# Windowed attention with a gated feed-forward layer on one core: the second product turned round, in blocks of 128 tokens over pairs of batches

## The chip, the cores and the metric

The kernel runs on one core of a Trainium2 chip. The core has a matrix engine (TensorE, PE in the profile, its weight loads PEld), three engines for elementwise work (VectorE = DVE, ScalarE = ACT, GpSimd = POOL) and a queue engine, SyncE (SP), that issues transfers. The metric is the device time in microseconds of one execution. The time before is the median of three runs, 547.44 us (547.39 to 547.52). The profile is of one execution, whose first and last instruction lie 546.0 us apart.

## What is computed

Eight batches of 576 tokens, eight heads of 64. The first four heads attend to the last 32 tokens, the others to every fourth of the last 128. The heads' outputs side by side are the input x (512 columns) of a feed-forward layer with 1024 inner columns:

```
def _attn_ref(q, k, v):                      # B, H, S, D = 8, 8, 576, 64
    scores = scale * np.matmul(q, k.transpose(0, 1, 3, 2))
    mask_plain = (rel >= 0) & (rel < window)                               # window 32
    mask_dil = (rel >= 0) & (rel < window * dilation) & (rel % dilation == 0)   # dilation 4
    attn = softmax(np.where(masks, scores, -1e9))
    return np.matmul(attn, v)

def _moe_ref(x, w_in, conv_w, w_out):        # x: 8 x 576 x 512, d_ff 1024
    h = np.maximum(x @ w_in, 0.0)
    conv_out = sum(conv_w[k] * hp[:, k:k + S, :] for k in range(3))   # hp: h with a zero at each end of the tokens
    gate = 1.0 / (1.0 + np.exp(-conv_out))
    return (h * gate @ w_out).astype(np.float32)
```

## The kernel before, in words

Work is cut into tasks, and a planner (class Planner, L76) puts them in order before the program is written. Each task has an engine, an estimated cost, a due time, a function that writes its instructions, the tasks that it comes after, and the buffers that it uses. The planner keeps a model of when each engine is free; among the tasks that could start within 0.25 us of the earliest on an engine it takes the one with the smallest due time. Due times are therefore priorities, and their scale matters only against each other. A buffer is taken from a pool of slots when its first task is placed and goes back when its last task is done. The order of each engine's instructions in the program is the order that comes out.

**Attention** (attention, L235) makes one task chain for each pair of heads, four pairs a batch. SP loads queries and keys (L243) and values (L245). PE forms the scores (L264) in the one accumulator "att"; for the first eight pairs a mask product goes ahead (L253), and VectorE and ScalarE make maxima and nine exponentials with their sums (L274 to L284); for the others VectorE adds the mask (L289, L292) and ScalarE makes one exponential (L298). VectorE normalizes and transposes (L305, L307), PE multiplies by the values (L318), and ScalarE and VectorE write the result as a high part (L368) and a rest (L384). Seven slots "x" hold these results, one pair each.

**The weights** (weights, L462) are split into a high part and a rest as well, in chunks of 128 x 512: eight of w_in, eight of w_out. GpSimd's queue loads the raw words into an "out" slot (L470), ScalarE and VectorE work on them (L477 to L512), and for nine chunks PE adds the parts (L499 to L501). The chunks' due times are WI and WO.

**The feed-forward layer** (expert, L391) runs once a batch. All its products take three matmuls for each chunk of the contraction: high by high, high by rest, rest by high (TERMS, L389).

- The first product (L402) has w_in stationary and 288 tokens moving: for each of the eight inner chunks fc and each half of the tokens, 4 x 3 matmuls into a PSUM slot "mm". ScalarE applies the relu and writes h (L409).
- Gating of chunk fc: ScalarE multiplies by the middle tap (L420), VectorE adds the other two (L414), ScalarE takes the sigmoid (L425), VectorE multiplies by h (L427), ScalarE writes the high part of the gated activations g (L429), VectorE the rest (L431). h and c have three slots each; g has eight, one for each chunk, so that a batch's g can be written only when the batch before has read that slot for the last time.
- The second product (L444) has w_out stationary and 288 tokens of g moving. For each of four blocks dm of 128 output columns and each half of the tokens, eight tasks k of three matmuls each run into a PSUM slot "nn" (two slots). Chunk 2 dm + k // 4 of w_out belongs to block dm, so a block needs two chunks of w_out and all eight of g. ScalarE copies the half out (L451), and SP stores a block of 128 x 576 (L458; for the last batch, each half by itself). The result lies transposed in memory, columns by tokens, and is put right on the host.

DUE gives each batch three due times, for the first product, the gating and the second product; PAIR gives one for each pair of heads; for batches 2 to 7 both follow a period of 57.4 us.

Of the kernel before, what the change touches and what calls it, by code (L numbers as in the profile page):

```python
# [8 lines left out]
F32 = mybir.dt.float32  # L36
F32R = mybir.dt.float32r
# [4 lines left out]
ALU = mybir.AluOpType  # L42
AX = mybir.AxisListType

B, H, S, D = 8, 8, 576, 64
DM, DF = 512, 1024
# [4 lines left out]
HALF = S // 2  # L51
RUNS = ((0, 5), (5, 9), (9, 14), (14, 18))
NC, NF = DM // 128, DF // 128
# [3 lines left out]
SCALE = 1.0 / D ** 0.5  # L57
ONE = dict(start=True, stop=True, skip_group_check=True)
# [101 lines left out]
def attn_moe(ctx: ExitStack, tc: tile.TileContext, qk_p, qk_d, v_p, v_d, w_in, w_out, conv, mask, out):  # L160
    nc = tc.nc
# [10 lines left out]
    wo = [[const.tile([128, 512], F32R, name=f"wo{j}{c}") for c in range(2 * NC)] for j in range(2)]  # L172
# [15 lines left out]
    slots("g", NF, [128, S], F32R, 2)  # L188
# [13 lines left out]
    AHEAD = (8.0, 4.1, 0.0)  # L202
# [186 lines left out]
    TERMS = ((0, 0), (0, 1), (1, 0))  # L389

    def expert(b, ready, wired, wored, conved):  # L391
        due, gated, out_due = DUE[b]
        x = [xs[b, p] for p in range(NP)]
        h, c, g = ([Buffer(n) for _ in range(NF)] for n in "hcg")
# [23 lines left out]
        for fc in range(NF):  # L418
            d = gated + 3.2 * fc
            t = plan.add("ACT", 0.777, d, lambda fc=fc: nc.scalar.activation(  # L420
                out=c[fc].t, in_=h[fc].t[:, 1:S + 1], func=AF.Copy, scale=conv_sb[:, 1, fc:fc + 1]),
                [relu[2 * fc], relu[2 * fc + 1], conved], [h[fc], c[fc]])
            for k in (0, 2):
                t = plan.add("DVE", 0.815, d + 0.5, lambda fc=fc, k=k: tap(fc, k), [t], [h[fc], c[fc]])
            t = plan.add("ACT", 0.686, d + 1.0, lambda fc=fc: nc.scalar.activation(  # L425
                out=c[fc].t, in_=c[fc].t, func=AF.Sigmoid), [t], [c[fc]], "sigmoid")
            t = plan.add("DVE", 0.755, d + 1.5, lambda fc=fc: nc.vector.tensor_tensor(  # L427
                out=c[fc].t, in0=c[fc].t, in1=h[fc].t[:, 1:S + 1], op=ALU.mult), [t], [c[fc], h[fc]])
            hi = plan.add("ACT", 0.675, d + 2.0, lambda fc=fc: nc.scalar.copy(out=g[fc].t[0], in_=c[fc].t),  # L429
                          [t], [c[fc], g[fc]])  # L430
            lo = plan.add("DVE", 0.755, d + 2.5, lambda fc=fc: nc.vector.tensor_tensor(  # L431
                out=g[fc].t[1], in0=c[fc].t, in1=g[fc].t[0].bitcast(F32), op=ALU.subtract), [hi], [c[fc], g[fc]])
            gates.append(lo)

        for dm in range(NC):
            o = Buffer("out")
            outs = []
            for hf in range(2):
                u = 2 * dm + hf
                ps, last = Buffer("nn"), None  # L440

                def second(dm, hf, ps, k):
                    for i, (jw, jg) in enumerate(TERMS):
                        nc.tensor.matmul(ps.t[:, 0:HALF], wo[jw][2 * dm + k // 4][:, k % 4 * 128:k % 4 * 128 + 128],  # L444
                                         g[k].t[jg][:, hf * HALF:hf * HALF + HALF],
                                         start=(k == 0 and i == 0), stop=(k == NF - 1 and i == 2))

                for k in range(NF):
                    last = plan.add("PE", 0.396, out_due + 3.3 * u + 0.4 * k, lambda a=(dm, hf, ps, k): second(*a),
                                    [last, wored[2 * dm + k // 4], gates[k]], [ps, g[k]], "E")  # L450
                outs.append(plan.add("ACT", 0.4, out_due + 3.3 + 3.3 * u, lambda hf=hf, ps=ps, o=o: nc.scalar.copy(  # L451
                    out=o.t[:, hf * HALF:hf * HALF + HALF], in_=ps.t[:, 0:HALF]), [last], [ps, o]))
                if b == B - 1:
                    plan.add("SP", 0.6, out_due + 4.0 + 3.3 * u, lambda dm=dm, hf=hf, o=o: nc.sync.dma_start(
                        out=out[b, dm, :, hf * HALF:hf * HALF + HALF], in_=o.t[:, hf * HALF:hf * HALF + HALF]),
                        [outs[-1]], [o])
            if b < B - 1:
                plan.add("SP", 1.2, out_due + 4.0 + 6.6 * dm, lambda dm=dm, o=o: nc.sync.dma_start(  # L458
                    out=out[b, dm], in_=o.t[:, :S]), outs, [o])
# [72 lines left out]
    wored = [weights(w_out[c], 512, WO[c], pair=(wo[0][c], wo[1][c]), summed=c < SUMMED - NF) for c in range(2 * NC)]  # L532
# [7 lines left out]
def _layouts(q, k, v, moe_w_in, moe_conv_w, moe_w_out):  # L540
# [28 lines left out]
    for hd in range(2):  # L569
# [28 lines left out]
        "w_out": w_out.reshape(2, 4, 128, NC, 128).transpose(3, 0, 2, 1, 4).reshape(2 * NC, 128, 512),  # L598
# [21 lines left out]
```

## Time and profile before

| | |
|---|---|
| median of 3 runs | 547.44 us (547.39 to 547.52) |
| the profiled execution, first to last instruction | 546.0 us; the page has no other time for it |
| mean granted TensorE clock | 0.991 |
| PE matmuls, weight loads | 8508 of each recorded |
| second product (L444), share of the chain that ended last | 36% |
| first product (L402), share of that chain | 32% |
| transfers | 52.29 MB, mean 96 GB/s |

Busy time is the sum of an engine's instruction times. Matmuls overlap in the array, so that one of 295 ns can start 0.13 us after the one before it. A group's row has its line, engine, operation, tiles and shapes and its count, then busy time and mean ns of one, then the engine's idle time ahead of them and what ended it. The chain that ended last goes back from the last instruction, step by step, to what released each. In the slices each digit is the busy share of a fortieth of the span, in tenths. Some matmul records are missing from the trace, so counts by the code can be a little above the recorded ones.

### The profile page before, as it was taken

What the parts mean: (1) busy time and instruction counts of PE and PEld (TensorE: products, weight loads), DVE (VectorE), ACT (ScalarE), POOL (GpSimd) and SP (SyncE); (2) the same over time, 40 slices, a digit from 0 to 9 for tenths busy, and PEclk for the clock granted to TensorE, in tenths of its full rate; (3) what the DMA queues carried; (4) which work ended last, traced back from release to release, by engine and by line L of the source; (5) the groups of instructions that cost most, each with busy time, mean ns of one, the idle gap of its engine ahead of it and who ended that gap; (6) DMA issues with size and microseconds to landing.
All of it is one profiled execution on the core that took longest, in us unless ns stands there. A gap on an engine that the chain in (4) does not pass through costs nothing.

```text
span 546.0 us, 18894 instructions
## 1 busy us (share of the span) xinstructions
PE 514.2 (94%) x8508; PEld 487.9 (89%) x8508; DVE 405.1 (74%) x692; ACT 301.0 (55%) x681; POOL 10.2 (2%) x29
## 2 busy tenths in 40 slices
PE   1668999999989999999999999999999999999997
PEld 1356888999979999999999999999999999999997
DVE  1878899998997389856998289856998289856920
ACT  3647799655742487237742577227743576237721
POOL 1100000000000000000000000000000000000000
PEclk9969999999999999999999999999999999999999
DMA  6656634022235102440045102440045102200011
GB/s 250 220 185 226 191 98 136 5 82 97 73 118 176 33 22 77 151 151 22 1 165 165 57 13 78 153 147 23 1 161 176 49 14 78 99 26 22 1 44 43
DMA packets 16959, 52.29 MB, mean 96 GB/s; under 512 B 1888, under 2 KB 3056, under 8 KB 16880
## 3 DMA queue, kind: packets, MB, share of 16 engines
q1 hardware_dynamic: 14400, 42.60, 23.7%
q0 software_dynamic: 2336, 8.41, 4.7%
q8 instruction: 66, 1.08, 0.8%
q10 hardware_dynamic: 144, 0.08, 0.1%
q14 instruction: 13, 0.11, 0.1%
HBM read 41.66 MB, written 9.44 MB: 94 GB/s over the span
## 4 chain that ended last, share of the span: by engine, by line
PE 80%; ACT 10%; DVE 7%; DMA 1%; issue 1%; POOL 0%; ACTq 0%; DVEq 0%; POOLq 0%
PE nn L444 36%; PE mm L402 32%; PE att L318 6%; PE att L264 5%; ACT s L284 4%; DVE c L414 2%; DMA out<-in_w_in_dram 1%; ACT c L420 1%; ACT h L409 1%; DVE m L274 1%; ACT c L425 1%; DVE c L427 1%; ACT L425 0%; DVE pt L307 0%; ACT w1a L477 0%
## 5 line engine op out<-in xcount | busy, mean ns | idle before, releaser
L414 DVE SCALAR_TENSOR_TENSOR c<-h,conv_sb,c 128x576 f32<-128x576 f32 x128 | 103.9, 815 | 37.8 <-ACT c L420 36.6
L409 ACT ACTIVATE h<-mm 128x288 f32<-128x288 f32 x120 | 48.9, 409 | 51.9 <-PE mm L402 51.7
L451 ACT COPY out<-nn 128x288 f32<-128x288 f32 x64 | 25.3, 398 | 71.0 <-PE nn L444 66.8
L427 DVE TENSOR_TENSOR c<-c,h 128x576 f32<-128x576 f32 x64 | 48.0, 754 | 14.4 <-ACT c L425 12.8
L318 PEld LDWEIGHTS att<-pt,v 32*64 32x64 f32 x2944 | 38.6, 135 | 14.7 <-ACT s L284 5.1
L318 PE MATMUL att<-pt,v 32*64 32x64 f32 (+2 forms) x2944 | 42.4, 230 | 8.4 <-ACT s L284 4.0
L420 ACT ACTIVATE c<-h,conv_sb 128x576 f32<-128x576 f32 x64 | 49.5, 775 | 1.1
L425 ACT ACTIVATE c<-c 128x576 f32<-128x576 f32 x64 | 43.4, 679 | 5.2 <-DVE c L414 4.4
L402 PE MATMUL mm<-x2a,wi 128*128 128x288 f32 x144 | 40.6, 297 | 0.7 <-ACT h L409 0.7
L402 PE MATMUL mm<-x0a,wi 128*128 128x288 f32 x144 | 40.4, 296 | 0.0
L402 PE MATMUL mm<-x3a,wi 128*128 128x288 f32 x144 | 40.3, 296 | 0.0
L402 PE MATMUL mm<-x1a,wi 128*128 128x288 f32 x144 | 40.3, 295 | 0.0
L444 PE MATMUL nn<-g0a,wo 128*128 128x288 f32 x128 | 37.3, 306 | 0.2
L264 PE MATMUL att<-qk 64*32 64x64 f32 x2432 | 35.4, 232 | 1.8 <-DVE s L292 1.4
L444 PE MATMUL nn<-g2a,wo 128*128 128x288 f32 x128 | 36.7, 302 | 0.0
L444 PE MATMUL nn<-g1a,wo 128*128 128x288 f32 x128 | 36.5, 300 | 0.0
L444 PE MATMUL nn<-g3a,wo 128*128 128x288 f32 x128 | 36.4, 299 | 0.0
L264 PEld LDWEIGHTS att<-qk 64*32 64x32 f32 x2432 | 29.7, 109 | 7.4 <-issue 4.1
L444 PE MATMUL nn<-g4a,wo 128*128 128x288 f32 x128 | 36.3, 299 | 0.0
L444 PE MATMUL nn<-g6a,wo 128*128 128x288 f32 x128 | 36.2, 299 | 0.0
L402 PE MATMUL mm<-x4a,wi 128*128 128x288 f32 x128 | 35.8, 295 | 0.0
L402 PE MATMUL mm<-x5a,wi 128*128 128x288 f32 x128 | 35.8, 295 | 0.0
(170 smaller groups left out, 1498.5 us busy)
## 6 DMA issues: line engine op xcount, KB each, us to landing
qk<-in_qk_d_dram SPq DMA_DIRECT2D x16, 664.0 KB, 4.7
qk<-in_qk_p_dram SPq DMA_DIRECT2D x16, 592.0 KB, 4.1
out_dram<-out SPq DMA_DIRECT2D x28, 288.0 KB, 2.1
v<-in_v_p_dram SPq DMA_DIRECT2D x16, 384.0 KB, 3.7
v<-in_v_d_dram SPq DMA_DIRECT2D x16, 384.0 KB, 3.5
out<-in_w_in_dram POOLq DMA_DIRECT2D x8, 512.0 KB, 4.0
out<-in_w_out_dram POOLq DMA_DIRECT2D x8, 512.0 KB, 3.9
out_dram<-out SPq DMA_DIRECT2D x8, 144.0 KB, 1.8
```

What stands on the lines that cost most here:

```text
L264: nc.tensor.matmul(sc.t[quad * 32:quad * 32 + 32, bank, c * W:c * W + W], q, k, start=i == 0 and not eased, stop=i == len(parts) - 1, skip ...
L274: last = plan.add("DVE", 0.68, due + 1.5, lambda: nc.vector.tensor_reduce(out=m.t.rearrange("p (h a) -> p h a", h=2)[:, :, 0:4], in_=banks ...
L284: nc.scalar.activation(out=s.t[:, i, :], in_=sc.t[:, bank, c * W:c * W + W], func=AF.Exp, scale=SCALE, bias=m.t[:, i:i + 1], accum_out=z.t ...
L318: nc.tensor.matmul(tv.t[hd * 64:hd * 64 + 64, bank, o:o + n], v.t[quad * 32:quad * 32 + 32, block // 2, block % 2 * 64:block % 2 * 64 + 64 ...
L402: nc.tensor.matmul(ps.t[:, 0:HALF], wi[jw][fc][:, k * 128:k * 128 + 128], x[k].t[jx][:, hf * HALF:hf * HALF + HALF], start=(k == 0 and i = ...
L409: relu.append(plan.add("ACT", 0.4, due + 1.6 * u + 1.6, lambda fc=fc, hf=hf, ps=ps: nc.scalar.activation(out=h[fc].t[:, 1 + hf * HALF:1 + ...
L414: nc.vector.scalar_tensor_tensor(out=c[fc].t, in0=h[fc].t[:, k:S + k], scalar=conv_sb[:, k, fc:fc + 1], in1=c[fc].t, op0=ALU.mult, op1=ALU ...
L420: t = plan.add("ACT", 0.777, d, lambda fc=fc: nc.scalar.activation(out=c[fc].t, in_=h[fc].t[:, 1:S + 1], func=AF.Copy, scale=conv_sb[:, 1, ...
L425: t = plan.add("ACT", 0.686, d + 1.0, lambda fc=fc: nc.scalar.activation(out=c[fc].t, in_=c[fc].t, func=AF.Sigmoid), [t], [c[fc]], "sigmoid")
L427: t = plan.add("DVE", 0.755, d + 1.5, lambda fc=fc: nc.vector.tensor_tensor(out=c[fc].t, in0=c[fc].t, in1=h[fc].t[:, 1:S + 1], op=ALU.mult ...
L444: nc.tensor.matmul(ps.t[:, 0:HALF], wo[jw][2 * dm + k // 4][:, k % 4 * 128:k % 4 * 128 + 128], g[k].t[jg][:, hf * HALF:hf * HALF + HALF], ...
L451: outs.append(plan.add("ACT", 0.4, out_due + 3.3 + 3.3 * u, lambda hf=hf, ps=ps, o=o: nc.scalar.copy(out=o.t[:, hf * HALF:hf * HALF + HALF ...
```

## The change

The second product changes its sides. A block of 128 tokens of g is now stationary, and 512 columns of w_out move: eight chunks k, three matmuls each, into a full PSUM slot. So that blocks of 128 tokens come out even, two batches share the eight g buffers, now 640 columns wide: the even batch writes columns 0 to 575, the odd one columns 64 to 639. The even batch has four blocks (its tokens 64 to 575). The odd one has five: the first takes the even batch's tokens 0 to 63, which still lie in columns 0 to 63, and its own first 64; four more follow. The odd batch's high part waits for the even batch's last block to have read that chunk (read). A chunk of w_out is now 128 rows with all 512 columns, one for each k, so a block needs all eight. The result is stored by tokens, with no transpose left on the host; the last block is copied and stored in two halves of 256 columns. All due times are given for each batch and chunk, and the scratch for GpSimd's transfer descriptors is set to 8192 bytes, where the program before leaves it unset.

```
+REST = S % 128
+DUE = {
+    0: (580.8, 27.9, -1.4),
+    1: (213.6, -299.0, 236.5),
+    2: (298.7, 74.3, 336.3),
...
+    7: (425.8, 381.5, 859.4),
+}
+PAIR = {
+    0: (-457.5, -556.4, -489.6, -298.9),
+    1: (-233.9, -88.4, -68.9, 30.4),
+    2: (100.4, 158.5, 106.2, 115.4),
...
+    7: (590.7, 577.9, 625.9, 591.3),
+}
+WI = (-419.2, 32.4, -71.8, -195.1, -259.0, 8.1, -51.2, -117.3)
+WO = (47.2, 77.7, 55.2, 78.0, 38.6, 19.0, 87.9, 102.0)
-    slots("g", NF, [128, S], F32R, 2)
+    slots("g", NF, [128, S + REST], F32R, 2)
-    DUE = {0: (-4.3, 1.8, 23.7), 1: (68.3, 34.2, 99.8)}
-    PAIR = {0: (-42.0, -47.4, -46.7, -32.4), 1: (-4.4, -28.5, -16.5, -5.9)}
-    WI, WO = (-21.6, -21.1, -2.7, -2.7, -3.0, -0.1, 7.2, 7.8), (10.5, 12.6, 37.1, 43.0, 43.8, 43.6, 51.6, 56.5)
-    PERIOD = 57.4
-    for b in range(2, B):
-        DUE[b] = tuple(t + PERIOD * b for t in (-5.3, 10.9, 32.3))
-        PAIR[b] = tuple(t + PERIOD * b for t in (-21.1, -18.7, -14.6, -13.5))
+        g = gs.setdefault(b // 2, [Buffer("g") for _ in range(NF)]) if b % 2 == 0 else gs[b // 2]
+        at = b % 2 * REST
+            gate = lambda fc, j: g[fc].t[j][:, at:at + S]
+            hi = plan.add("ACT", 0.675, d + 2.0, lambda fc=fc: nc.scalar.copy(out=gate(fc, 0), in_=c[fc].t),
+                          [t, read.get((b - 1, fc)) if b % 2 else None], [c[fc], g[fc]])
...
+        blocks = [(0, [(0, (b - 1) * S, REST), (REST, b * S, REST)])] if b % 2 else []
+        blocks += [(at + t, [(0, b * S + t, 128)]) for t in range(REST, S, 128)]
+        for u, (first_col, rows) in enumerate(blocks):
+            o, ps, last = Buffer("out"), Buffer("nn"), None
+            def second(col, ps, k):
+                for i, (jw, jg) in enumerate(TERMS):
+                    nc.tensor.matmul(ps.t, g[k].t[jg][:, col:col + 128], wo[jw][k],
+                                     start=(k == 0 and i == 0), stop=(k == NF - 1 and i == 2))
+            for k in range(NF):
+                last = plan.add("PE", 0.693, out_due + 5.6 * u + 0.7 * k, lambda a=(first_col, ps, k): second(*a),
+                                [last, wored[k], gates[k]], [ps, g[k]], "E")
+                if b % 2 == 0:
+                    read[b, k] = last
+            last_one = b == B - 1 and u == len(blocks) - 1
+            halves = [(0, 256), (256, 512)] if last_one else [(0, 512)]
+            for c0, c1 in halves:
+                t = plan.add("ACT", 0.16 + 0.00093 * (c1 - c0), out_due + 5.6 + 5.6 * u, ...copy to o...)
+                for p0, row, n in rows:
+                    plan.add("SP", 0.6, out_due + 5.8 + 5.6 * u, ...store rows row to row + n...)
-        "w_out": w_out.reshape(2, 4, 128, NC, 128).transpose(3, 0, 2, 1, 4).reshape(2 * NC, 128, 512),
+        "w_out": w_out.reshape(NF, 128, DM),
-    nc = bacc.Bacc("TRN2", target_bir_lowering=False, num_devices=1)
+    nc = bacc.Bacc("TRN2", target_bir_lowering=False, num_devices=1, dynamic_dma_scratch_size=8192)
```

More of the change, by code (lines that the diff above doesn't have):

```diff
@@ L57 @@
 SCALE = 1.0 / D ** 0.5
+DUE = {
+    0: (580.8, 27.9, -1.4),
+    1: (213.6, -299.0, 236.5),
+    2: (298.7, 74.3, 336.3),
+    3: (207.5, 235.5, 370.3),
+    4: (392.2, 246.5, 569.0),
+    5: (236.9, 118.2, 411.6),
+    6: (240.1, 311.5, 692.5),
+    7: (425.8, 381.5, 859.4),
[4 more added lines that the diff above has]
+    2: (100.4, 158.5, 106.2, 115.4),
+    3: (159.5, 176.7, 263.5, 224.6),
+    4: (271.0, 337.4, 174.1, 173.0),
+    5: (406.9, 395.3, 384.0, 446.3),
+    6: (231.2, 489.6, 330.6, 394.1),
+    7: (590.7, 577.9, 625.9, 591.3),
+}
+WI = (-419.2, 32.4, -71.8, -195.1, -259.0, 8.1, -51.2, -117.3)
+WO = (47.2, 77.7, 55.2, 78.0, 38.6, 19.0, 87.9, 102.0)
+AHEAD = (8.0, 4.1, 0.0)
 ONE = dict(start=True, stop=True, skip_group_check=True)
@@ L171, in attn_moe @@
     wi = [[const.tile([128, 512], F32R, name=f"wi{j}{c}") for c in range(NF)] for j in range(2)]
-    wo = [[const.tile([128, 512], F32R, name=f"wo{j}{c}") for c in range(2 * NC)] for j in range(2)]
+    wo = [[const.tile([128, DM], F32R, name=f"wo{j}{c}") for c in range(NF)] for j in range(2)]
     plan = Planner()
@@ L196, in attn_moe @@
     slots("nn", 2, [128, 512], pool=psum)
-    DUE = {0: (-4.3, 1.8, 23.7), 1: (68.3, 34.2, 99.8)}
-    PAIR = {0: (-42.0, -47.4, -46.7, -32.4), 1: (-4.4, -28.5, -16.5, -5.9)}
-    WI, WO = (-21.6, -21.1, -2.7, -2.7, -3.0, -0.1, 7.2, 7.8), (10.5, 12.6, 37.1, 43.0, 43.8, 43.6, 51.6, 56.5)
-    AHEAD = (8.0, 4.1, 0.0)
-    PERIOD = 57.4
-    for b in range(2, B):
-        DUE[b] = tuple(t + PERIOD * b for t in (-5.3, 10.9, 32.3))
-        PAIR[b] = tuple(t + PERIOD * b for t in (-21.1, -18.7, -14.6, -13.5))
     SUMMED = 9
@@ L389, in attn_moe @@
     TERMS = ((0, 0), (0, 1), (1, 0))
+    gs, read = {}, {}
     def expert(b, ready, wired, wored, conved):
@@ L393, in expert @@
         x = [xs[b, p] for p in range(NP)]
-        h, c, g = ([Buffer(n) for _ in range(NF)] for n in "hcg")
+        h, c = ([Buffer(n) for _ in range(NF)] for n in "hc")
+        g = gs.setdefault(b // 2, [Buffer("g") for _ in range(NF)]) if b % 2 == 0 else gs[b // 2]
+        at = b % 2 * REST
         relu = []
@@ L428, in expert @@
                 out=c[fc].t, in0=c[fc].t, in1=h[fc].t[:, 1:S + 1], op=ALU.mult), [t], [c[fc], h[fc]])
-            hi = plan.add("ACT", 0.675, d + 2.0, lambda fc=fc: nc.scalar.copy(out=g[fc].t[0], in_=c[fc].t),
-                          [t], [c[fc], g[fc]])
+            gate = lambda fc, j: g[fc].t[j][:, at:at + S]
+            hi = plan.add("ACT", 0.675, d + 2.0, lambda fc=fc: nc.scalar.copy(out=gate(fc, 0), in_=c[fc].t),
+                          [t, read.get((b - 1, fc)) if b % 2 else None], [c[fc], g[fc]])
@@ L431, in expert @@
             lo = plan.add("DVE", 0.755, d + 2.5, lambda fc=fc: nc.vector.tensor_tensor(
-                out=g[fc].t[1], in0=c[fc].t, in1=g[fc].t[0].bitcast(F32), op=ALU.subtract), [hi], [c[fc], g[fc]])
+                out=gate(fc, 1), in0=c[fc].t, in1=gate(fc, 0).bitcast(F32), op=ALU.subtract), [hi], [c[fc], g[fc]])
             gates.append(lo)
[L435 to L459, printed above, removed]
@@ new lines, in expert @@
+        blocks = [(0, [(0, (b - 1) * S, REST), (REST, b * S, REST)])] if b % 2 else []
[14 more added lines that the diff above has]
+            for c0, c1 in halves:
+                t = plan.add("ACT", 0.16 + 0.00093 * (c1 - c0), out_due + 5.6 + 5.6 * u, lambda ps=ps, o=o, c0=c0, c1=c1: nc.scalar.copy(
+                    out=o.t[:, c0:c1], in_=ps.t[:, c0:c1]), [last], [ps, o])
+                for p0, row, n in rows:
+                    plan.add("SP", 0.6, out_due + 5.8 + 5.6 * u, lambda o=o, p0=p0, row=row, n=n, c0=c0, c1=c1: nc.sync.dma_start(
+                        out=out[row:row + n, c0:c1], in_=o.t[p0:p0 + n, c0:c1]), [t], [o])
@@ L531, in attn_moe @@
     conved = weights(conv, 3 * NF, -4.0, dst=conv_sb.rearrange("p t c -> p (t c)"))
-    wored = [weights(w_out[c], 512, WO[c], pair=(wo[0][c], wo[1][c]), summed=c < SUMMED - NF) for c in range(2 * NC)]
+    wored = [weights(w_out[c], 512, WO[c], pair=(wo[0][c], wo[1][c]), summed=c < SUMMED - NF) for c in range(NF)]
     for b in range(B):
@@ L613 @@
         args.append(nc.dram_tensor(f"in_{name}_dram", a.shape, mybir.dt.from_np(a.dtype), kind="ExternalInput").ap())
-    args.append(nc.dram_tensor("out_0_dram", (B, NC, 128, S), F32, kind="ExternalOutput").ap())
+    args.append(nc.dram_tensor("out_0_dram", (B * S, DM), F32, kind="ExternalOutput").ap())
     with tile.TileContext(nc) as tc:
@@ L618 @@
     got = r.results[0]["out_0_dram"]
-    return np.ascontiguousarray(got.reshape(B, DM, S).transpose(0, 2, 1))
+    return np.ascontiguousarray(got).reshape(B, S, DM)
```

## The prediction

> **What bounds the kernel now.** I read the page's busy times first, then the slices, then the chain that ended last.
>
> ```profile
> PE 514.2 (94%) x8508; PEld 487.9 (89%) x8508; DVE 405.1 (74%) x692; ACT 301.0 (55%) x681; POOL 10.2 (2%) x29
> PE   1668999999989999999999999999999999999997
> DVE  1878899998997389856998289856998289856920
> PEclk9969999999999999999999999999999999999999
> PE 80%; ACT 10%; DVE 7%; DMA 1%; issue 1%; POOL 0%; ACTq 0%; DVEq 0%; POOLq 0%
> PE nn L444 36%; PE mm L402 32%; PE att L318 6%; PE att L264 5%; ACT s L284 4%; DVE c L414 2%; DMA out<-in_w_in_dram 1%; ACT c L420 1%; ACT h L409 1%; DVE m L274 1%; ACT c L425 1%; DVE c L427 1%; ACT L425 0%; DVE pt L307 0%; ACT w1a L477 0%
> ```
>
> TensorE is busy nearly throughout, at nearly full granted clock, and 80% of the chain is its work. The two products share it: the second (L444) has 36% of the span. A mean over the span hides stages, so I asked for the busy time of four stretches (columns: stretch, length, then busy time and instructions of PE, PEld, DVE, ACT, POOL, granted clock, DMA share, GB/s).
>
> ```profile
> 10.00:40.00 30.00, 19.60 (x561) 13.19 (x565) 22.14 (x53) 15.72 (x72) 2.64 (x5) 0.83 0.58 192
> 40.00:94.00 54.00, 49.00 (x1054) 42.10 (x1048) 48.93 (x98) 46.61 (x154) 3.28 (x6) 1.00 0.52 166
> 94.00:155.00 61.00, 59.40 (x573) 58.38 (x572) 57.47 (x92) 36.78 (x69) 1.70 (x3) 1.00 0.19 59
> 155.00:516.00 361.00, 360.16 (x6149) 349.10 (x6149) 271.34 (x446) 190.95 (x367) 0.00 (x0) 1.00 0.25 82
> ```
>
> From 155 to 516 us PE is idle for 0.84 of 361 us while VectorE works 75% of the time: there every nanosecond of matmul is a nanosecond of the kernel. From 94 to 155 both PE (1.6 us idle) and VectorE (3.5 us idle) are full: gating of two batches, attention and the weights' splitting meet there. Before 94 PE waits: 5.0 us between 40 and 94, and 10.4 us between 10 and 40, on the first attention pairs. So the change is priced on PE's own time, then checked for what it does to the stretch up to 155, where order and VectorE matter.
>
> **The matmuls.** The busy durations of single matmuls overlap and can't be added, so I price by start-to-start distance. In the timeline and the chain of waits, a 288-column matmul:
>
> ```profile
> 303.36 0.29 PE L402 MATMUL mm<-x1a,wi 128*128 128x288 f32 x1
> 303.49 0.29 PE L402 MATMUL mm<-x1b,wi 128*128 128x288 f32 x1
> 250.83 19.08 PE mm L402 x144
> 312.28 19.08 PE mm L402 x144
> ```
>
> 19.08 us / 144 = 0.1325 us each. L444 has the same shape, and its count is eight chunks, each with the high part twice and the low part once (first group of the eight pairs, from the groups by shape):
>
> ```profile
> L444 PE MATMUL nn<-g0a,wo 128*128 128x288 f32 x128 | 37.3, 306 | 0.2
> L444 PE MATMUL nn<-g0b,wo 128*128 128x288 f32 x64 | 18.9, 296 | 0.0
> ```
>
> So 8 x (128 + 64) = 1536 matmuls, 203.5 us (37% of 546.0; the chain says 36%). The change has 9 blocks per pair of batches, 8 chunks, 3 terms: 216 per pair, 864 in all, each of 512 columns. The number of columns is the same, 1536 x 288 = 864 x 512 = 442,368; what goes is 672 matmuls and as many weight loads. The price of one of 512 columns isn't in the steady part, but the weights' splitting has some with the same operand type (L501), and the start of whatever follows each is in the timeline:
>
> ```profile
> 75.82 0.39 PE L501 MATMUL nn<-wi,minus 128*128 128x512 f32 x1
> 76.05 1.02 PE L499 MATMUL nn<-w0b,ident 128*128 128x512 f32 x2
> 77.14 0.39 PE L501 MATMUL nn<-wi,minus 128*128 128x512 f32 x1
> 77.37 0.29 PE L402 MATMUL mm<-x3a,wi 128*128 128x288 f32 x1
> 81.77 0.39 PE L501 MATMUL nn<-wo,minus 128*128 128x512 f32 x1
> 82.00 0.30 PE L402 MATMUL nn<-x3a,wi 128*128 128x288 f32 x1
> ```
>
> Three times 0.23 us, the last digit being 0.01. I take 0.230: 864 x 0.230 = 198.7 us, a **saving of 4.8 us**. For the bounds I allow 5 ns either way: 0.225 saves 9.1 us, 0.235 saves 0.5 us (a price in proportion to columns, 0.1325 x 512/288 = 0.2356, saves 0). Between 288 and 512 columns that is 0.435 ns a column and about 7 ns that don't depend on width; these 7 ns, 672 times, are the 4.8 us.
>
> Beside this stands a rule that speaks against the change. The Trainium skill ("TensorE: Matmul & The Clock Gate", section "Back-to-back issue gap") gives an isolated gap of N/2.4 + 2.5 ns: 122.5 ns at 288 columns and 215.8 at 512, so an estimate of 672 x 2.5 ns = 1.7 us saved. The trace agrees with neither figure (132.5 and 230), so I keep the rows; the case in which the rule is right about the difference is a rival below.
>
> **Around the matmuls.** The result is copied out by ScalarE; its present rows, and the nearest rows for the new widths (512 and 256 columns from PSUM), then the end of the run:
>
> ```profile
> L451 ACT COPY out<-nn 128x288 f32<-128x288 f32 x64 | 25.3, 398 | 71.0 <-PE nn L444 66.8 <-DMA qk<-in_qk_d_dram 1.4 <-DVE w0a L490 1.1
> L504 ACT CAST wi<-nn 128x512 fp32r<-128x512 f32 x8 | 4.9, 611 | 2.5 <-PE nn L501 2.5
> L368 ACT CAST x0a<-att 128x256 fp32r<-128x256 f32 x3 | 1.2, 387 | 4.5 <-DVE s L296 3.5 <-PE att L318 1.1
> 521.49 0.77 DVE g7b L431
> 523.32 19.35 PE nn L444 x144
> 542.37 0.29 PE L444 MATMUL nn<-g7a,wo 128*128 128x288 f32 x1
> 542.74 0.40 ACT L451 COPY out<-nn 128x288 f32<-128x288 f32 x1 [2.79 <-PE nn L444]
> out_dram<-out SPq DMA_DIRECT2D x28, 288.0 KB, 2.1
> out_dram<-out SPq DMA_DIRECT2D x8, 144.0 KB, 1.8
> ```
>
> Copies: 64 x 0.398 = 25.5 us become 35 x 0.611 + 2 x 0.387 = 22.2 us, on an engine that is 53% busy in the steady stretch: worth nothing, covered by the 5.5 us that the other accumulator's block takes (24 x 0.23); without that cover it would be 0.6 us a block. At the very end the cover is gone: two copies of 256 columns stand where one of 288 did, 2 x 0.387 - 0.398 = **+0.4 us**. The last store shrinks from 144 to 128 KB, which I count at nothing. SP issues 41 stores instead of 36, spread over the run; loads for attention queue behind a store that waits for its copy, as they do now. POOL's halved descriptor scratch I also set at nothing: the weight loads on that queue already wait for a free raw buffer; if it does bite, a chunk arrives one landing (4 us) later, early in the run.
>
> The end by itself: after the last gate (521.49) PE does 150 of 288 columns now (six whole units and 2 x 3 left of the two that accumulate), 19.9 us; then three whole blocks and 2 x 3, 78 x 0.23 = 17.9 us. These 2 us are part of the 4.8, if gating isn't later.
>
> The new wait: the copy into the odd batch's gates waits until the even batch's last block has read that chunk. Behind it on ScalarE stand relus and copies out, and the relus' release of PSUM is what the first product waits for. But the single set of eight gate buffers makes it wait now as well, for the last unit, which lasts 24 x 0.1325 = 3.2 us; a last block lasts 5.5 us, so chunk 0 comes free 2.3 us earlier before the product's end. No cost, perhaps a little slack.
>
> **The due times** change the order of everything. They can add no PE time; they can close or open idle time. At best they close what is idle from 40 to 155, 5.0 + 1.6 = 6.6 us; the 10.4 before 40 hang on the first pairs' latency, which no order shortens much. At worst they lose 8.0 us around w_out (below). I take **-2 us**, some third of what can be closed, since VectorE, 91% and 94% busy in these two stretches, leaves little.
>
> Sum: -4.8 + 0.4 - 2 = -6.4 us. The span is 546.0; the median of the runs, 547.44, stands 1.4 us above it (launch and end outside the first and last instruction), and this remains: **541.0 us**.
>
> **The rivals.**
>
> *Slower: w_out comes too late.* Now two chunks of w_out are enough for the first 128 output columns. After the change the first block needs all eight. When they arrive, and what they hold up:
>
> ```profile
> L512 DVE TENSOR_TENSOR wo<-w0b,wo x4: 686/692/692, 89.9 to 134.3; 128x512 fp32r<-128x512 f32 x4
> 126.20 8.35 PE nn L444 x63
> 134.58 0.69 ACT g0a L429
> 153.37 0.68 DVE g7b L431
> ```
>
> The last chunk is ready at 135.0; batch 1's first gate is written at 134.58, and the gating behind it runs to 154. If that chunk stayed there, the two accumulators would stand at their last chunk: 6 matmuls, then a whole block of 24, then 3 until gate buffer 0 is free, 33 x 0.23 = 7.6 us, at 142.6 instead of 134.6. Gating is full there and PE has little else, so +8.0 us: 547.4 - 4.8 + 0.4 + 8.0 = 551.0. It decides from a delay of 4.4 us on, that is if w_out is done after some 131.4 us. For it: gating of batch 1 is due at -299, ahead of w_out (19 to 102), on a VectorE that is full. Against it: batch 0's relus, now due before six of the eight w_out chunks, are due at 582 and later in the change, so they give way and w_out is split while that batch's first product runs. 14%.
>
> *No gain from width.* The time goes by columns alone (0.2356 us), or the order gives back the 4.8 us; with the due times at 0, 547.4 + 0.4 = 547.8. For it: the column count is unchanged. Against: three times 0.23. 10%. By the skill's rule above it would be 547.4 - 1.7 + 0.4 = 546.1.
>
> *More than forecast.* 0.225 us a matmul and all 6.6 us of idle closed: -9.1 - 6.6 + 0.4 = -15.3, 532.1 us. For it: gaps of PE between 40 and 94 hang on scores and exponentials of single pairs, beside which other matmuls could run. Against: VectorE is nearly full. I give 8% to below 535.
>
> **How the numbers follow.** Forecast 541.0, own range 535 to 546, 68%; more 8%; no gain 10%; slower 14%. About 0.2% (1.1 us) is what a measurement of this kernel can tell from no change. Faster: 68 + 8 and a share of the "no gain" case, 78%; same 9%; slower 13%. The range takes the first case with most of the second and third: 533 to 550.
>
> **What would show it.** Right: after 155 us PE still without idle; 512-column matmuls 0.230 us apart, and 864 of them at about 198.7 us; the stretch from the last gate to the last matmul near 18 us; w_out complete well before 131 us. Wrong: a spacing of 0.235 or more; PE idle over 2 us between 94 and 155 that ends with a w_out chunk or gate; DVE's gating ending after 154 us in batch 1; the last gate after the previous block's work has run out.

## The result, and the profile after

The changed kernel takes **542.36 us** (median of four runs, 541.73 to 544.50) against 547.48 us for the kernel before beside it (547.39 to 548.21): ratio 0.990, 95% interval 0.988 to 0.992, so 5.1 us faster. The forecast was 541.0 us in a range of 533 to 550. The profiled execution took 542.24 us; its span is 540.4 us, 5.6 less than the 546.0 before. (The forecast kept 1.4 us between span and median; it is now 1.9, which is the half microsecond between 5.6 and 5.1.)

The page after: busy times, three slices' rows, and the chain that ended last.

```profile
PE 509.5 (94%) x7836; PEld 442.1 (82%) x7836; DVE 400.1 (74%) x692; ACT 310.0 (57%) x662; POOL 10.3 (2%) x29
PE   1678997999999999999999999999999999999997
DVE  0999999899999789986893479985869309847910
PEclk9889997899999999999999999999999999999999
PE 75%; DVE 13%; ACT 9%; DMA 1%; issue 1%; ACTq 0%; POOL 0%; POOLq 0%; DVEq 0%
PE nn L440 33%; PE mm L398 30%; PE att L309 6%; PE att L255 4%; ACT s L275 4%; DVE c L410 3%; DMA out<-in_w_in_dram 1%; DVE s L296 1%; DVE pt L298 1%; DVE c L423 1%; PE nn L495 1%; DVE m L265 1%; ACT c L421 1%; ACT c L416 1%; ACT L289 0%
```

There are exactly 672 fewer matmul records (8508 to 7836), and weight loads fell from 89% to 82% of the span. The second product is now L440, with 33% of the chain instead of 36%. VectorE has more of the chain than before (13% against 7%). In the clock's row a 7 and an 8 stand at the seventh and eighth slice, 81 to 108 us, where the kernel before had full clock. The stretches, as in the prediction (stretch, length, then PE, PEld, DVE, ACT, POOL, clock, DMA share, GB/s):

```profile
10.00:40.00 30.00, 20.77 (x520) 12.51 (x520) 25.04 (x56) 18.53 (x81) 2.65 (x5) 0.90 0.61 201
40.00:94.00 54.00, 47.09 (x1124) 41.44 (x1125) 49.85 (x103) 46.39 (x151) 3.38 (x6) 0.94 0.49 162
94.00:155.00 61.00, 60.87 (x604) 52.49 (x591) 57.20 (x95) 35.73 (x62) 1.69 (x3) 0.96 0.25 83
155.00:516.00 361.00, 360.25 (x5522) 318.99 (x5522) 267.97 (x441) 202.50 (x358) 0.00 (x0) 1.00 0.24 78
```

PE is idle for 0.75 us between 155 and 516, about as before (0.84). Between 94 and 155 it lost 1.6 us to waits before and loses 0.1 now, but between 40 and 94 it loses 6.9 instead of 5.0. Next the new matmul, from the chain's last long pieces and two neighbours of the timeline, and the end of the run (ScalarE's two copies are shown as one row):

```profile
509.30 27.22 PE nn L440 x120
```
```profile
535.89 0.39 PE L440 MATMUL nn<-wo,g7b 128*128 128x512 f32 x1
536.12 0.39 PE L440 MATMUL nn<-wo,g7a 128*128 128x512 f32 x1
536.59 0.65 ACT L451 COPY out<-nn 128x256 f32<-128x256 f32 x2 [4.85 <-PE nn L440]
```

120 matmuls in 27.22 us are **0.2268 us each**, where the forecast took 0.230: 864 x 0.2268 = 196.0 us, 7.6 less than 203.5, not 4.8. From the start of the last matmul to the end of the span it is 540.4 - 536.12 = 4.3 us, 546.0 - 542.37 = 3.6 before: +0.65. At these prices, taken from undisturbed rows, -7.6 + 0.65 = -6.95 is the second product's own part, and 1.35 us of the span came back elsewhere. They were lost early: at 155 us 118 of 864 second-product matmuls are done (13.7%) against 241 of 1536 (15.7%), 2.0% or 4.0 us behind; one group of scores and one of values more are done, some 2.2 us. Net about 1.8 us behind, near the 1.35.

The split depends on the price. Added up over the whole trace from the start of each matmul to the start of the next, with waits and steps to other work included, the second product fell from 216.7 to 205.4 us, 11.3 less. The first product rose by 2.9 us (210.6 to 213.5), the weights' matmuls by 5.2 (19.5 to 24.7), and attention fell by 3.5 (85.7 to 82.2). So 7.6 is what undisturbed rows give; in the whole kernel the second product gained more, and more was lost early.

More views, for the prediction's signs: the w_out chunks' last step (first and last start after the counts), batch 1's first and last high part from ScalarE's timeline, and the last gate of the run:

```profile
L508 DVE TENSOR_TENSOR wo<-w0b,wo x5: 681/684/691, 56.8 to 130.9; 128x512 fp32r<-128x512 f32 x5
```
```profile
139.37 0.68 ACT L426 CAST g0a<-c 128x576 fp32r<-128x576 f32 x1
160.05 0.67 ACT L426 CAST g7a<-c 128x576 fp32r<-128x576 f32 x1 [0.83 <-DVE c L423]
```
```profile
515.07 0.76 DVE L428 TENSOR_TENSOR g7b<-c,g7a 128x576 fp32r<-128x576 f32 x1 [0.74 <-ACT g7a L426]
```

The last chunk is ready at 131.6 instead of 135.0 us. Batch 1's gates are nevertheless written 4.8 us later than before (139.37 against 134.58), and the last of them 7.6 us later (160.05; before, 152.48). So two of the prediction's signs went against it, w_out well before 131 us and batch 1's gating done by 154, and PE still loses nothing between 94 and 155. A third sign missed too: from the end of the last gate (515.83) to the start of the last matmul (536.12) it is 20.3 us, not near 18, and before it was 20.1 (522.25 to 542.37). That stretch did not shrink, but PE runs its last 120 matmuls without a break from 509.3 us on, so it never waits for that gate and the missed sign costs nothing.

The same stretch around the low clock, before first, then after, with the columns of the stretches above:

```profile
86.00:100.00 14.00, 13.20 (x175) 12.56 (x175) 13.65 (x23) 12.64 (x24) 0.04 (x1) 1.00 0.30 97
```
```profile
86.00:100.00 14.00, 11.09 (x286) 9.32 (x287) 12.76 (x22) 9.92 (x21) 0.53 (x1) 0.63 0.44 145
```

After, the mean granted clock is 0.63 there and PE is idle 2.9 us of 14. PE's digits alone hide this loss, since a slow matmul counts as busy too. Two rows of the chain show it: nine first-product matmuls there take 0.273 us each, and the 132 that follow 0.1324.

```profile
94.72 2.46 PE mm L398 x9
...
101.60 17.48 PE mm L398 x132
```

### The profile page after: what moved, and what is told of

The parts are those of the page before. It is cut to its first block, busy times and chain, and to the rows that moved or that the text cites. A ratio compares the mean times of both kernels' runs of the same rounds, so it can differ in the third digit from the quotient of the medians.

```text
span 540.4 us, 17510 instructions
## 1 busy us (share of the span) xinstructions
PE 509.5 (94%) x7836; PEld 442.1 (82%) x7836; DVE 400.1 (74%) x692; ACT 310.0 (57%) x662; POOL 10.3 (2%) x29
## 4 chain that ended last, share of the span: by engine, by line
PE 75%; DVE 13%; ACT 9%; DMA 1%; issue 1%; ACTq 0%; POOL 0%; POOLq 0%; DVEq 0%
PE nn L440 33%; PE mm L398 30%; PE att L309 6%; PE att L255 4%; ACT s L275 4%; DVE c L410 3%; DMA out<-in_w_in_dram 1%; DVE s L296 1%; DVE pt L298 1%; DVE c L423 1%; PE nn L495 1%; DVE m L265 1%; ACT c L421 1%; ACT c L416 1%; ACT L289 0%
## 5 line engine op out<-in xcount | busy, mean ns | idle before, releaser
L451 ACT COPY out<-nn 128x512 f32<-128x512 f32 (+1 forms) x37 | 21.1, 572 | 64.5 <-PE nn L440 61.7
L398 PE MATMUL mm<-x3a,wi 128*128 128x288 f32 x176 | 49.7, 297 | 0.0
L421 ACT ACTIVATE c<-c 128x576 f32<-128x576 f32 x64 | 42.5, 681 | 11.4 <-DVE c L410 10.7
L398 PE MATMUL mm<-x4a,wi 128*128 128x288 f32 x160 | 45.7, 300 | 0.1
L398 PE MATMUL mm<-x6a,wi 128*128 128x288 f32 x128 | 36.1, 297 | 0.0
L398 PEld LDWEIGHTS mm<-x3a,wi 128*128 128x128 f32 x176 | 33.0, 188 | 0.4
L398 PE MATMUL mm<-x0a,wi 128*128 128x288 f32 x112 | 31.6, 298 | 0.0
L291 DVE TENSOR_REDUCE z<-s 128x9 f32<-128x576 f32 x24 | 17.9, 748 | 18.2 <-ACT s L289 18.1
L398 PEld LDWEIGHTS mm<-x4a,wi 128*128 128x128 f32 x160 | 30.2, 189 | 0.9 <-ACT h L405 0.5
L440 PE MATMUL nn<-wo,g5a 128*128 128x512 f32 x72 | 28.9, 402 | 0.0
L440 PE MATMUL nn<-wo,g4a 128*128 128x512 f32 x72 | 28.9, 402 | 0.0
```

What stands on the lines that cost most here:

```text
L291: last = plan.add("DVE", 0.755, due + 3.5, lambda: nc.vector.tensor_reduce(out=nine(z.t), in_=nine(s.t), axis=AX.X, op=ALU.add), [last], [ ...
L398: nc.tensor.matmul(ps.t[:, 0:HALF], wi[jw][fc][:, k * 128:k * 128 + 128], x[k].t[jx][:, hf * HALF:hf * HALF + HALF], start=(k == 0 and i = ...
L440: nc.tensor.matmul(ps.t, g[k].t[jg][:, col:col + 128], wo[jw][k], start=(k == 0 and i == 0), stop=(k == NF - 1 and i == 2))
L451: t = plan.add("ACT", 0.16 + 0.00093 * (c1 - c0), out_due + 5.6 + 5.6 * u, lambda ps=ps, o=o, c0=c0, c1=c1: nc.scalar.copy(out=o.t[:, c0:c ...
```

## The experiments

The kernel before ran beside each; its medians were 547.92 us in the first group (first four experiments), 548.19 in the second, 547.89 in the third.

**The changed kernel once more, unchanged.**

> The changed kernel once more, unchanged, beside the others on the same chip: 541.5 to 544.5 us by its first four runs. Theory of the cold stretch: it is a consequence of the order (TensorE waits four times between 79 and 94 us), so its granted clock falls to 0.5 near 90 us here too. Rival: the fall is a chance of the clock's window, and another run has it elsewhere or not at all, which would explain the first runs' spread of 2.8 us.

Measured: 543.35 us (541.90 to 543.83), ratio 0.991 (0.989 to 0.994). The stretch from 86 to 100 us:

```profile
86.00:100.00 14.00, 11.19 (x287) 9.42 (x288) 12.77 (x22) 9.91 (x19) 0.53 (x1) 0.63 0.45 145
```

It is the same stretch with the same clock, 0.63. The fall belongs to this order, not to chance. Over both sets, eight runs of the changed kernel lie at 541.73 to 544.50.

**All due times as before.** The turned product stays; DUE, PAIR, WI and WO are those of the kernel before.

```
-DUE = {0: (580.8, 27.9, -1.4), ...}      -PAIR = {...}      -WI, WO = ...
+DUE = {0: (-4.3, 1.8, 23.7), 1: (68.3, 34.2, 99.8)}
+PAIR = {0: (-42.0, -47.4, -46.7, -32.4), 1: (-4.4, -28.5, -16.5, -5.9)}
+WI, WO = (-21.6, -21.1, -2.7, ...), (10.5, 12.6, 37.1, 43.0, 43.8, 43.6, 51.6, 56.5)
+for b in range(2, B): DUE[b], PAIR[b] = the old pattern with period 57.4
```

> The turned second product with every due time of the kernel before (DUE, PAIR, WI, WO). Theory: two terms that are independent. The matmuls save 1536 x 0.1325 - 864 x 0.2268 = 7.6 us in any order, and the longer end costs 0.65 us; but the first block now needs all eight w_out chunks, and in the old order the last one is ready at about 135 us, which holds batch 1's gating back by up to 8 us: 547.5 - 7.6 + 0.65 + 8 = 548.5 us, with the last w_out chunk at 133 to 137 us and batch 1's first gate after 140. Rival (the order of w_out doesn't matter, other work covers it, and the new due times are mere adjustment): 547.5 - 7.6 + 0.65 = 540.5 us. If the new due times lost time in the changed kernel (its early part is some 1 us behind), it would come out even below 542.

Measured: **551.49 us** (550.59 to 552.76), ratio 1.006 (1.004 to 1.008): slower than the kernel before. PE's waits between 94 and 155 us (total, times, longest), and the w_out chunks' last step:

```profile
PE nn L425 <- ACT wo L492: 5.1, 2, 3.5
PE mm L383 <- ACT h L390: 0.7, 1, 0.7
```
```profile
L493 DVE TENSOR_TENSOR wo<-w0b,wo x4: 684/688/693, 91.0 to 134.7; 128x512 fp32r<-128x512 f32 x4
```

The last chunk is ready at 135.4, as the prediction's slower rival had it, PE stands 5.1 us for w_out, and batch 1's gates begin after 143 us. The total also has three waits for relus after 155 us (1.6 us at most, 2.9 together). The time is 3.0 us above the 548.5 expected, which had no relu waits in it. So the turned product with the old order loses what it gains and more; the new due times are worth 8.1 us to it.

**Matmuls of 256 columns.** Each of the second product's matmuls is cut in two. Both halves open their sum in the same PSUM slot, and the kernel loses contributions by it: its output is off by 0.25 (relative error). That fits a second opening that discards what the first half had just received, one chunk of eight in half of the columns (estimated as the square root of 1/16, 0.25). The matmuls are otherwise those of the changed kernel, twice as many.

```
-                    nc.tensor.matmul(ps.t, g[k].t[jg][:, col:col + 128], wo[jw][k], ...)
+                    for c in (0, 256):
+                        nc.tensor.matmul(ps.t[:, c:c + 256], g[k].t[jg][:, col:col + 128], wo[jw][k][:, c:c + 256], ...)
```

> The changed kernel, each matmul of the second product cut into two of 256 columns with a weight load each (1728 instead of 864; same columns, same order). Theory: a matmul costs 0.421 ns a column and a fixed 11.3 ns (fitted to 132.5 ns at 288 and 226.8 at 512): 256 columns take 119 ns, 864 more fixed costs make +9.8 us: about 552 us. Rival: at 288 columns the weight load sets the 132.5 ns, so that no narrower matmul can come faster: 1728 x 0.1325 = 229 us, +33 us: about 575 us. Second rival (time goes by columns alone): 0 us, 542.

Measured: 550.54 us (median of ten; 549.64 to 554.82), ratio 1.004 (1.002 to 1.006). The chain's last long piece, and the chain by engine:

```profile
515.38 28.80 PE nn L441 x240
```
```profile
PE 85%; DVE 6%; ACT 5%; DMA 1%; issue 1%; POOL 0%; ACTq 0%; POOLq 0%; DVEq 0%
```

28.80 / 240 = 0.1200 us: the fixed cost (0.119 expected), not the weight load's 0.1325 and not columns alone (0.1134). With three widths the price is 0.120, 0.1325 and 0.2268 us at 256, 288 and 512 columns: 0.42 ns a column and 11 to 13 ns each. Per pair of halves that is 13.2 ns, 864 times 11.4 us; the total rose by 7.2 only, and by 7.7 between the profiled spans (548.1 and 540.4). The traces show where the rest is. From start to next start, as above, the second product takes 213.8 us instead of 205.4, 8.4 more: about 10 ns for each matmul added, less than in an undisturbed row. And attention takes 0.7 us less, which shows in the values between 40 and 94 us (9.3 instead of 10.0), where the clock fell less far:

```profile
86.00:100.00 14.00, 10.31 (x289) 8.67 (x290) 12.66 (x22) 10.37 (x22) 0.53 (x1) 0.76 0.44 145
155.00:516.00 361.00, 360.81 (x6126) 351.49 (x6126) 263.59 (x435) 199.55 (x355) 0.00 (x0) 1.00 0.24 78
```

8.4 - 0.7 is the 7.7 us. PE is idle for 0.2 us after 155 here and 0.75 in the changed kernel, so there the time still goes by PE's matmuls, as the prediction had it. VectorE's smaller share of the chain (6%, against 13%, and 10% in the repeated run) says nothing against that.

**Fillers near 80 to 94 us.** 38 matmuls that no one reads, ahead of four steps of attention; in this first form each also opens a sum in a bank that holds partial sums of the first product, and part of these is lost (the output is off by 0.04).

```
+    FILL, turn = {13: 8, 14: 4, 15: 20, 16: 6}, [0]
+    def fill():
+        for _ in range(FILL.get(turn[0], 0)):
+            nc.tensor.matmul(mms[0][0][:, 288:512], ones, mask_sb[:, 0, 0:224], **ONE)
+        turn[0] += 1
...
         def scores():
+            fill()
...
         def values():
+            fill()
```

> The changed kernel with 38 matmuls of no use (224 columns, bf16, into columns of a PSUM slot that nothing reads), placed ahead of the scores and values of the four pairs' steps near 80 to 93 us, where TensorE waits for them and its granted clock then fell to 0.5 for some 10 us. Theory: the low clock costs about 3.4 us there, since some 8 us of matmuls run at half speed: clock near 1.00 from 88 to 100 us, total about 539 us. Rival: VectorE sets the pace in that stretch (57 of 61 us busy from 94 to 155), so the clock costs nothing: 542 us. If the clock stays low the run tells nothing of its price.

Measured: 541.39 us (540.82 to 541.79), ratio 0.987 (0.985 to 0.989). The clock was 1.00 from 80 to 102 us. The profiled span is 539.9 us, and that of the unchanged kernel 540.0: no gain between the two profiles, while the medians differ by 2.0. But the unchanged kernel's profile is of the fastest of its four runs (541.90; the others 543.18 to 543.83) and this one of the slowest (541.79), so the two spans don't decide it. The expected 3.4 us did not come.

**The same fillers without touching the sums** (start=False once the first product has begun):

> The changed kernel with the fillers ahead of four steps at 79 to 94 us alone (38 matmuls), the result not touched: the other part of the fillers' gain. Theory as in the run with fillers at the same places: 541.4 us, runs within 1 us. If the gain is in the first pairs: 542 to 543.5.

Measured: 541.51 us (540.68 to 543.40), ratio 0.987 (0.984 to 0.990); span 540.1. Its interval overlaps that of the unchanged kernel (0.989 to 0.994), so this part alone is unclear, and the four runs do not lie within 1 us.

**Fillers in nine waits from 12 us on:**

```
+    FILL, turn = {1: 34, 2: 12, 5: 26, 6: 12, 9: 6, 13: 8, 14: 4, 15: 20, 16: 6}, [0]
```

> The changed kernel with matmuls of no use (224 columns, bf16) in nine of TensorE's waits ahead of the first pairs' scores and values, from 12 to 94 us; the result is not touched by them. Theory: the granted clock stays near 1.00 from 12 us on. In the run with fillers near 80 to 94 us alone, the profiled span was 539.9 us against 540.0 without, but its four runs lay at 540.8 to 541.8 against 541.9 to 543.8. If cold stretches only spread the runs (each waits elsewhere for a warm clock), these runs lie within 1.0 us of each other and near 541.0. If a warm clock ahead of 50 us also shortens the first pairs (half-speed scores and w_in sums there, some 8 us of PE work), 539.5 to 540.5. Rival: no price on the path, the first four runs' difference was chance: 542 to 544.

Measured: **540.95 us** (539.21 to 541.10), ratio 0.985 (0.982 to 0.988), the fastest of all; all four runs lie below all eight of the changed kernel. The two stretches that were cold, with the columns as above; for the second, the changed kernel's row first (its row for the first is above, 0.63):

```profile
28.00:40.00 12.00, 8.66 (x170) 4.54 (x170) 10.84 (x26) 8.18 (x34) 1.60 (x3) 0.89 0.56 189
```
```profile
86.00:100.00 14.00, 13.11 (x331) 11.18 (x330) 13.25 (x23) 12.02 (x25) 0.53 (x1) 1.00 0.46 145
28.00:40.00 12.00, 10.43 (x206) 7.28 (x206) 11.31 (x26) 7.99 (x37) 1.71 (x3) 1.00 0.64 217
```

The clock is 1.00 in both, and batch 1's last high part comes at 158.5 instead of 160.0: about 1.5 us won by there. The medians differ by 2.4 us from the repeated run and 1.4 from the first four.

**Fillers in the kernel before:** the same fill() with {1: 34, 2: 9, 3: 14, 4: 17, 5: 14, 7: 5, 8: 12}.

> The kernel before with 105 matmuls of no use (224 columns, bf16) in TensorE's waits ahead of seven of the first pairs' steps, 12 to 52 us; the result is not touched. In the changed kernel such fillers made 540.95 us of 543.35. Theory: the gain belongs to the cold clock of the first pairs, which the kernel before has too (0.5 from 30 to 39 us): about 1.5 us, 546 us. Rival: the gain is the stretch at 88 to 99 us that only the changed kernel has; then nothing here, 547.5 to 548.2, and the two orders differ by these 2 us.

Measured: 546.37 us (545.36 to 551.68), ratio 0.997 (0.993 to 1.001). Four of five runs are at 545.4 to 546.4, below all but one of the kernel before beside them (546.4 to 550.2), but with the fifth the interval reaches over 1: likely 1.5 us, not shown. If so, the gain of fillers is not a merit of either order.

**Batch 0's first product put back to -4.3,** one number.

```
-    0: (580.8, 27.9, -1.4),
+    0: (-4.3, 27.9, -1.4),
```

> The changed kernel with one due time put back: batch 0's first product at -4.3 instead of 580.8, so that its relus go ahead of w_out again. Theory (the argument of the prediction): the relus push w_out back, its last chunk comes later than 131.5 us, batch 1's first gate later than 140.0, and each microsecond of that costs one: about 546 us with the last chunk near 134. The gap of TensorE at 88 to 90 us shrinks, since the first product gets its PSUM slots back sooner. Rival: ScalarE has room for both, the chunk stays at 131 to 132 us and the time at 542 to 543.5.

Measured: **561.70 us** (560.42 to 562.65), ratio 1.024 (1.020 to 1.027). The w_out chunks' last step, and PE's longest wait between 94 and 155:

```profile
L508 DVE TENSOR_TENSOR wo<-w0b,wo x4: 683/684/693, 58.0 to 125.7; 128x512 fp32r<-128x512 f32 x4
```
```profile
PE nn L440 <- ACT wo L507: 12.2, 1, 12.2
```

The direction was right and the reason wrong: w_out is complete at 126.4, earlier than in the changed kernel, yet PE stands 12.2 us, from 99.9 to 112.1, for w_out's second chunk in the order of k: both accumulators hold the first one's sums and go through the chunks in a fixed order. Nothing else can run. Batch 0's first product is over (its last matmul starts at 96.0 us; in the changed kernel at 85.5), and batch 1's cannot begin: it needs all four pairs, and two still lack their values. These need the one accumulator "att". Here the scores of a pair of batch 2 go into it first, at 85.6 us; VectorE, busy with gating and w_out, reads them from 119.1 us on, and only then come the values, at 121.4 and 124.5:

```profile
85.58 1.37 PE L255 MATMUL att<-qk 64*32 64x64 f32 x72 [4.82 <-ACT s L275]
119.11 0.68 DVE L280 TENSOR_TENSOR s<-att,mask_sb 128x512 f32<-128x512 f32 x1
121.44 1.36 PE L309 MATMUL att<-pt,v 32*64 32x64 f32 x96
```

In the changed kernel these two values stand ahead of those scores, so that batch 1's first product runs from 91.6 us on and fills PE while w_out is split:

```profile
86.16 1.36 PE L309 MATMUL att<-pt,v 32*64 32x64 f32 x96 [0.38 <-ACT s L275]
89.65 2.06 PE L309 MATMUL att<-pt,v 32*64 32x64 f32 x96 [2.13 <-DVE x6b L375]
```

The last chunk's time is not what sets the total.

**w_out later by 100:** all eight due times in WO raised.

> The changed kernel with w_out's eight due times later by 100. Theory: w_out sets when batch 0's blocks end and batch 1's gates can be written, so with the last chunk at T the time is 543.3 + (T - 131.5) us, with TensorE waiting for w_out chunks ahead of the second product; for T near 145, 557 us. Rival: attention of batch 2 and batch 1's first product fill the wait and the time rises by less than half of that, below 550.

Measured: 577.69 us (575.75 to 578.09), ratio 1.052 (1.049 to 1.056). The last chunk's last step starts at 176.3 us and ends at 177.0; then PE's waits for w_out, all after 155 us, and its longest between 94 and 155:

```profile
L508 DVE TENSOR_TENSOR wo<-w0b,wo x4: 680/687/693, 98.1 to 176.3; 128x512 fp32r<-128x512 f32 x4
PE nn L440 <- ACT wo L507: 7.8, 4, 2.2
PE att L244 <- ACT s L275: 10.1, 1, 10.1
```

The chunk is 45.4 us later and the time 34.3 us longer, 0.76 for one; the rival that other work would fill the wait falls, and one for one (589 us) is too much. Nor is w_out what PE mostly waits for: until 155 us it waits for steps of attention, which this order has moved too.

**w_out earlier by 6:**

> The changed kernel with w_out's eight due times earlier by 6. Theory A (w_out's last chunk sets the time, one for one): the chunk comes earlier, batch 1's first gate before 140.0, and the time falls below 542. Theory B (what counts is the time of batch 1's first gate, and the due times fit only as a set; any shift pushes something else back, as in the run with batch 0's first product put forward, whose chunk came at 126 and whose gate came at 157): slower, 545 to 555, with the first gate later than 140.0 by about as much as the time rises.

Measured: 555.07 us (554.41 to 555.73), ratio 1.011 (1.009 to 1.014). Between 94 and 155 us PE waits for exponentials and for a rest of x, not for w_out; batch 1's first and last high part in the timeline:

```profile
PE att L309 <- ACT s L275: 5.3, 1, 5.3
PE att L309 <- DVE x6b L375: 1.6, 1, 1.6
```
```profile
140.39 0.68 ACT L426 CAST g0a<-c 128x576 fp32r<-128x576 f32 x1
175.34 0.68 ACT L426 CAST g7a<-c 128x576 fp32r<-128x576 f32 x1 [1.89 <-DVE c L423]
```

Theory A falls. Theory B is right that it gets slower, but the first gate is only 1 us later; it is the last that moves, by 15.3 us, with the total 11.7 to 12.7. Here too batch 1's last two values come late, at 103.1 and 106.8 us.

**Batches 2 to 7 by the old pattern,** the rest new:

```
+for b in range(2, B):
+    DUE[b] = tuple(t + 57.4 * b for t in (-5.3, 10.9, 32.3))
+    PAIR[b] = tuple(t + 57.4 * b for t in (-21.1, -18.7, -14.6, -13.5))
```

> The changed kernel with the due times of batches 2 to 7 taken from the kernel before (period 57.4 us); batches 0 and 1 and the weights keep the new ones. Splits the 8.1 us between the changed kernel (543.35) and the same with all old due times (551.5), of which the trace shows 5.1 us as waits for w_out before 135 us and 3.6 us as waits for batch 3, 5 and 7's relus in mid-run. Theory: the early part is what counts, and this kernel keeps w_out on time: 5 of the 8 us stay, about 546.5 us, with the relu waits (0.7 to 1.6 us each) back. Rival: the later batches' order is what counts: 549 or more, with w_out still at 131 to 132 us.

Measured: 555.90 us (554.43 to 556.25), ratio 1.013 (1.010 to 1.016). Neither expectation holds: the time is the rival's (549 or more), but w_out is not at 131 to 132 us. Batch 2's pairs, at 93.7 to 101.3 in the old pattern, go ahead of w_out's last chunk, due at 102 (three groups of scores start between 128 and 136 us, where the changed kernel has one); that chunk slips to 141.1 us, PE waits 3.6 us for it between 94 and 155, and 3.1 us for scores' steps on VectorE:

```profile
PE nn L443 <- ACT wo L510: 3.6, 1, 3.6
PE att L258 <- DVE s L286: 3.1, 2, 1.9
```

**GpSimd's descriptor scratch set to 8192 bytes, in the kernel before:** `dynamic_dma_scratch_size=8192`.

> The kernel before with the halved scratch for GpSimd's transfer descriptors alone. Theory: nothing, within 0.2% of the kernel before, since the raw weights wait for a free slot anyway. Rival: chunks arrive one landing (4 us) later in the first 60 us, +1 to +4 us.

Measured: 547.71 us (median of ten; 546.61 to 548.39), ratio 0.999 (0.998 to 1.001): nothing.

The orders of the turned product, side by side (each from its own profile; idle of PE from the stretches and waits, high parts on ScalarE):

| | last w_out chunk | batch 1's first product, first and last start | batch 1's last high part starts | PE idle 94 to 155 | clock 94 to 155 | time |
|---|---|---|---|---|---|---|
| changed kernel | 131.6 | 91.6, 154.7 | 160.1 | 0.1 | 0.96 | 542.36, 543.35 |
| all due times old | 135.4 | 94.1, 157.1 | 162.9 | 5.4 | 0.97 | 551.49 |
| w_out earlier by 6 | 132.7 | 108.8, 168.9 | 175.3 | 8.0 | 0.86 | 555.07 |
| batches 2 to 7 old | 141.1 | 91.9, 167.4 | 172.9 | 6.7 | 0.86 | 555.90 |
| batch 0's first product at -4.3 | 126.4 | 139.8, 175.7 | 182.1 | 13.6 | 0.89 | 561.70 |
| w_out later by 100 | 177.0 | 119.5, 199.9 | 205.0 | 13.1 | 0.75 | 577.69 |

The total doesn't go with the w_out chunk. It goes roughly with the end of batch 1's first product and with the gates behind it. Each slower order shows PE idle between 94 and 155 us, and all but the old order a lower clock there too. The old order adds waits after 155 to that (4.2 us idle instead of 0.75), w_out later by 100 still more (9.8); this one and batch 0's first product at -4.3 also idle longer between 40 and 94 (12.2 and 10.4 us instead of 6.9).

## Why the prediction was right, step by step

**PE bounds it, matmuls are priced by distance.** Right in kind. The fixed cost per matmul is real and is what is saved; the experiment with 256 columns, which doubled the matmuls at the same columns, cost 7.2 us. The size was off: 0.2268 us and 7.6 us saved, inside the stated 0.225 to 0.235, against 0.230 and 4.8. The rows used had a last digit of 0.01 us, 4% of the price and nearly twice the difference looked for. A proportional price, the second rival, is excluded. The Trainium skill ("TensorE: Matmul & The Clock Gate", section "Back-to-back issue gap") gives the isolated gap a fixed part of 2.5 ns; the trace does not agree, its rows give 11 to 13 ns.

**Around the matmuls.** The end costs 0.65 instead of 0.4 us. The copies are 35 of 583 ns on the mean (611 assumed), and cost nothing; the scratch costs nothing, as measured alone in the kernel before. The stretch from the last gate on did not shrink by the 2 us that the prediction saw there, and since PE did not wait for that gate, nothing was lost by it.

**The due times: the term that failed.** The prediction took -2 us for them, as a third of the idle time that they could close. Against the kernel before the early part gave back about 1.4 us instead. Idle time from 94 to 155 was closed, as the term said, and 1.2 us before 40 with it, but 1.9 us were lost from 40 to 94. In sum PE is idle for 16.3 us between 10 and 155 instead of 17.0. So idle time, the measure that the term was taken from, fell a little and still time was lost; what the rows show besides is a cold stretch of some 10 us that came with the new order. The two misses, at the prices of undisturbed rows 2.8 us more saved by matmuls and 3.4 us less by order, nearly cancel: 541.0 forecast, 542.4 measured. Part of this closeness is luck.

They were also priced apart from the turned product, as an adjustment between -6.6 and +8 us. In truth the turned product without any of them is slower than the kernel before (551.49), and four smaller changes of them cost 12 to 34 us.

**The slower rival.** Its mechanism and its price are shown by the kernel with the old order: last chunk at 135.4, PE waiting for w_out, 551.49 us where the rival said 551.0 us; some of that time comes from later relu waits, which it did not have. Its point of decision failed. With a chunk after 131.4 us, or gates 4.4 us late, it was to use up the whole gain; the chunk came at 131.6 and batch 1's gates 4.8 us late, and still nothing was lost between 94 and 155. "PE has little else" was the wrong step. After the change PE goes through 132 matmuls of batch 1's first product in one piece, from 101.6 us, and then takes scores and values of batch 2 between the blocks; what is late is the second product, and PE does it after 155 us without idle time.

**The reason given against the rival** (batch 0's relus give way to w_out) was tested by the one-number change: it is slower, but w_out comes earlier then, not later. That argument is refuted. By the traces the number changes which task takes the accumulator "att" first, batch 1's last values or batch 2's scores, and with it whether PE has batch 1's first product to do while w_out is split. No run changes that order alone.

**The cold clock** was not in the prediction. Its price was estimated at 3.4 us from the half-speed matmuls; the fillers show less, 1.4 to 2.4 us in the medians for all the waits from 12 us on, and for the stretch at 88 to 99 alone 2.0 us between medians but nothing between the profiled spans (539.9 and 540.0). How much of the 1.35 us lost early is the clock and how much the waits between 40 and 94 is not settled.

## What to carry to other kernels

Price a matmul by start-to-start distance over a long row, at two widths: slope and intercept, times the matmuls that go, give the gain, here 11 to 13 ns for each of 672. When a change makes one step need all chunks of something where it needed two, the order must be made anew with it, and order and change can't be priced apart: ask what work each engine has in reserve while it waits, and which buffer that work needs. And read the granted clock beside the busy digits, since a busy engine at half clock hides its loss.

## What the runs showed of the hardware

- Matmuls of 128 x 128 stationary in this operand type, each with a weight load of its own: 0.1200 us at 256 columns, 0.1325 at 288, 0.2268 at 512, so 0.42 ns a column and 11 to 13 ns each in undisturbed rows. Going from 288 to 256 columns still shortened the distance, so at 288 it was not the weight load that set it, though one is shown as 188 ns.
- A step from such a matmul to the small ones of attention took longer than the row's distance: 0.222 us after 288 columns, 0.329 after 512 and 0.209 after 256 (means of 46, 32 and 32 steps from 155 to 516 us), 0.09 to 0.10 us more.
- The granted clock fell to 0.5 at 88.7 us, for 10.2 us, after waits of PE of 0.9, 0.4 and 2.1 us within some 10 us (mean 0.63 from 86 to 100 us), without one long wait, and in the same place in two profiles. Matmuls of no use in these waits kept it at 1.00.
